# A 2 KB output by two DMAs of neighbouring partitions instead of one DMA of four strided partitions

## The chip, the cores and the metric

The kernel runs on one core of one Trainium2 chip. The time is device time in microseconds (us) of that core; medians of several executions are given. "Span" is the time from the first to the last instruction in the profiled execution; it is some 1.8 us shorter than the device time. Times inside a span count from its start. A run is called fast when it is not over 1.5% above the fastest of its kernel; all the runs below are, but where a kernel ran only once its state is unknown.

Engines: TensorE (PE), VectorE (DVE), ScalarE (ACT), GpSimd (POOL) and SyncE (SP). DMAs are issued here by SyncE (queue q1 in the trace) and by ScalarE (queue q10).

## The reference, cut to what matters

One token goes through attention over a long cache and through a gated MLP, and a gate mixes the two:

```python
x = A_x                                              # (1, 1, 1024)
g = sigmoid((x * gate_w).sum(-1, keepdims=True))
a = A_ref(x, A_k_cache, A_v_cache, A_wq, A_wo)       # 32 heads, 4 kv heads, 65536 keys
b = B_ref(x, B_w_in, B_w_sp, B_b_sp, B_w_out)
return g * a + (1 - g) * b                           # (1, 1, 1024), bfloat16: 2 KB
```

All the inputs that are read come to 162 MB. The output is 2 KB.

## The kernel before

The last product, with `A_wo`, is accumulated in one tile `out_ps` of PSUM (the memory that TensorE writes its products to), of 128 partitions by 256 columns. The 1024 outputs are cut into four blocks of 256; block t fills partitions 32t to 32t+31, and all 32 partitions of a block hold the same values, because the vector is broadcast to 32 columns of weights.

```python
P, B, NB = 128, 32, 4
WO_SPLIT = ((16,), (8, 4, 2, 1, 1))     # columns of A_wo per load
...
NO = D // NB                            # 256
out_ps = psl.tile([P, NO], FP32, name="out_ps")

def project(w, n, vec, c0, first=False, last=False):
    for c in range(n):
        for t in range(NB):
            nc.tensor.matmul(
                out_ps[t * B:(t + 1) * B, :],
                lhsT=vec[:, c0 + c:c0 + c + 1].to_broadcast([P, B]),
                rhs=w[:, c, t * NO:(t + 1) * NO], ...)
...
for split in WO_SPLIT:
    ...
    for n in split:
        nc.sync.dma_start(out=t[:, c0 - b:c0 - b + n, :], in_=wo_view[:, c0:c0 + n, :])
        project(t[:, c0 - b:c0 - b + n, :], n, oa, c0, last=(c0 + n == OC))
        c0 += n
out_sb = const.tile([P, NO], BF16, name="out_sb")
nc.scalar.copy(out=out_sb[:], in_=out_ps[:])
nc.scalar.dma_start(out=out.rearrange("o t (q n) -> (o t q) n", n=NO), in_=out_sb[::B, :])
```

`out_sb[::B, :]` takes partitions 0, 32, 64 and 96: one row of each block, 512 B each. After that nothing is left but the program's closing waits, drains and barriers.

Of the kernel before, what the change touches and what calls it, by code (L numbers as in the profile page):

```python
# [17 lines left out]
B = 32  # L18
# [9 lines left out]
def kernel(  # L28
# [15 lines left out]
    nc = tc.nc  # L44
# [127 lines left out]
    for t in range(2):  # L172
        nc.vector.tensor_tensor(
            out=xm[:, t], in0=xb_ps[:, t * P:(t + 1) * P].rearrange("p (i c) -> p c i", c=KC),
# [51 lines left out]
    for hf in range(2):  # L226
        nc.vector.tensor_tensor(  # L227
            out=zm[:, hf], in0=z_ps[:, hf * HN:hf * HN + ZN].rearrange("p (j c) -> p j c", c=FC),
# [3 lines left out]
                            in_=zm.rearrange("p h j c -> p h c j"), axis=AX.X, op=ALU.add)  # L232
# [44 lines left out]
    for k in range(NHB):  # L277
        xs = slice(k * NX // NHB, (k + 1) * NX // NHB)
        nc.vector.tensor_tensor(  # L279
            out=qm[:, xs], in0=q_ps[:, k * HN:(k + 1) * HN].rearrange("p (x j e) -> p x j e",  # L280
                                                                   j=B, e=2),
# [6 lines left out]
        out=q4[:], in0=q1[:].rearrange("p x e -> p (x e)").unsqueeze(1).to_broadcast(  # L288
            [P, NB, NX * 2]),
# [7 lines left out]
    for g in range(G):  # L297
        k, t0 = g * T2 // NB, g * T2 % NB
        nc.vector.tensor_copy(out=qs[:, g].rearrange("p b (t h) -> p b t h", t=T2),
                              in_=qv[:, k, t0:t0 + T2].rearrange("p t h b -> p b t h"))  # L300
# [107 lines left out]
    NO = D // NB  # L408
# [35 lines left out]
    for split in WO_SPLIT:  # L444
        t = kv.tile([P, CT * P], BF16, name="wo_t", tag="kv")
        t = t[:].rearrange("p (c n) -> p c n", n=D)
        b = c0
        for n in split:
            nc.sync.dma_start(out=t[:, c0 - b:c0 - b + n, :], in_=wo_view[:, c0:c0 + n, :])  # L449
            project(t[:, c0 - b:c0 - b + n, :], n, oa, c0, last=(c0 + n == OC))  # L450
            c0 += n
    out_sb = const.tile([P, NO], BF16, name="out_sb")
    nc.scalar.copy(out=out_sb[:], in_=out_ps[:])  # L453
    nc.scalar.dma_start(out=out.rearrange("o t (q n) -> (o t q) n", n=NO), in_=out_sb[::B, :])

    last = {}
    for ins in list(nc.cur_bb.bb.instructions):
# [36 lines left out]
```

## Time and profile before

| | before |
|---|---|
| device time, median | 385.78 us (385.75 to 385.80) |
| span of the profiled run | 383.92 us |
| load queue q1, share of 16 engines | 98.5% |
| from the start of the last cast to the end of the span | 2.90 us, 0.75% of the time |

From the page of the kernel before: the row of DMA busy tenths over 40 slices of the span, the load queue, and the chain that ended last by engine.

```profile
DMA  8999999999999999999999999999999999999995
q1 hardware_dynamic: 6192, 162.01, 98.5%
DMA 60%; DVE 20%; PE 11%; issue 5%; ACT 2%; SPq 1%; DVEq 0%; ACTq 0%
```

The kernel is bound by its loads until its last slice. Only there does anything else count. The end of the timeline of the kernel before (start us, duration us, engine, line, operation, what ended the idle time before it; ACTq is ScalarE's sequencer, issuing a DMA):

```profile
380.69 0.29 PE L414 MATMUL out_ps<-wo_t,oa 128*32 128x256 bf16 x4 [0.36 <-DMA wo_t<-in_A_wo_dram]
381.02 0.37 ACT L453 CAST out_sb<-out_ps 128x256 bf16<-128x256 f32 x1 [47.61 <-PE out_ps L414]
381.43 0.61 ACTq L454 DMA_DIRECT2D out_dram<-out_sb  x1
```

The last load's matmuls are followed by the cast, and that by one issue of 0.61 us. From the waits of SyncE's queue, before (what was waited for, total us, times, longest us):

```profile
SPq L489 <- DMA out_dram<-out_sb: 2.4, 1, 2.4
```

SyncE holds the program open until the output has landed. The packet and landing records of the trace split this end.

These are ScalarE's first four DMAs, of 8, 8, 1 and 1 rows:

```profile
0.74 0.61 ACTq L117 DMA_DIRECT2D xg<-in_A_x_dram  x1
1.39 0.29 ACTq L118 DMA_DIRECT2D xg<-in_gate_w_dram  x1
1.71 0.27 ACTq L120 DMA_DIRECT2D wb<-in_B_w_sp_dram  x1
2.00 0.27 ACTq L121 DMA_DIRECT2D wb<-in_B_b_sp_dram  x1
```

### The profile page before, as it was taken

The numbers are of one execution on the slowest core, as the hardware profiler recorded it, in microseconds if no ns is written. First come the engines' busy times: TensorE is split into PE (matmuls) and PEld (weight loads), VectorE is DVE, ScalarE is ACT, GpSimd is POOL, SyncE is SP. The second block draws the span as 40 slices with busy tenths as digits, with TensorE's granted clock in tenths as the row PEclk, the third lists the DMA queues.
The fourth block names the chain that finished last, engine by engine and source line by source line (L and its number), as shares of the span: only waits on it lengthen the run. The fifth ranks groups of instructions, "written<-read, shape, count | busy, mean of one in ns | idle before, by whom it ended". The sixth has DMA issues, their size and how long they took to land.

```text
span 383.9 us, 2650 instructions
## 1 busy us (share of the span) xinstructions
PE 242.3 (63%) x1372; PEld 59.3 (15%) x796; DVE 218.5 (57%) x211; ACT 39.6 (10%) x55; POOL 4.4 (1%) x10
## 2 busy tenths in 40 slices
PE   0433447976449948466699393774993937685553
PEld 0110001111202201011121020121220201121122
DVE  5141478988497563658975545679754546730040
ACT  1010001100511101014011010140110101400000
POOL 4000000000000000000000000000000000000000
PEclk9996559889659989686599797865997869888868
DMA  8999999999999999999999999999999999999995
GB/s 335 430 437 437 435 434 430 423 431 426 428 427 437 435 430 437 427 434 430 423 432 427 437 437 422 430 434 437 427 425 427 437 438 427 425 430 431 434 411 203
DMA packets 6248, 162.18 MB, mean 422 GB/s; under 512 B 728, under 2 KB 732, under 8 KB 1116
## 3 DMA queue, kind: packets, MB, share of 16 engines
q1 hardware_dynamic: 6192, 162.01, 98.5%
q8 instruction: 8, 0.13, 0.1%
q14 instruction: 4, 0.03, 0.0%
q10 hardware_dynamic: 44, 0.01, 0.0%
HBM read 162.01 MB, written 0.00 MB: 422 GB/s over the span
## 4 chain that ended last, share of the span: by engine, by line
DMA 60%; DVE 20%; PE 11%; issue 5%; ACT 2%; SPq 1%; DVEq 0%; ACTq 0%
DMA kn<-in_A_k_cache_dram 47%; DVE kt L320 16%; DMA wo_t<-in_A_wo_dram 8%; PE s_ps L326 8%; DMA win_t<-in_B_w_in_dram 5%; DVE pt L362 2%; PE o_ps L372 2%; ACT sc L337 1%; PE z_ps L213 1%; ACT sc L359 1%; DVE mx L341 1%; DVE o_sb L387 0%; SPq L449 0%; ACT L359 0%; PE nb_ps L352 0%
## 5 line engine op out<-in xcount | busy, mean ns | idle before, releaser
L326 PE MATMUL s_ps<-kt,wt 128*128 128x512 bf16 x512 | 142.3, 437 | 67.9 <-DVE kt L320 67.3
L320 DVE STREAM_TRANSPOSE kt<-kn 128x2048 int32<-128x2048 int32 x64 | 143.3, 2284 | 63.5 <-DMA kn<-in_A_k_cache_dram 63.4
L372 PE MATMUL o_ps<-vt,pt 128*64 128x512 bf16 x512 | 69.2, 432 | 8.8 <-DMA vt<-in_A_v_cache_dram 8.8
L326 PEld LDWEIGHTS <-wt 128*128 128x128 bf16 x256 | 27.6, 108 | 184.0 <-issue 122.9
L337 ACT CAST sc<-s_ps 128x1024 bf16<-128x1024 f32 x16 | 16.2, 1013 | 253.8 <-PE s_ps L326 253.8
L372 PEld LDWEIGHTS <-pt 128*64 128x64 bf16 x256 | 17.2, 124 | 57.9 <-issue 56.4
L362 DVE STREAM_TRANSPOSE pt<-sc 128x1024 bf16<-128x1024 bf16 x16 | 18.6, 1218 | 6.8 <-ACT sc L359 6.8
L383 DVE TENSOR_TENSOR om<-o_ps,own 128x1024 f32<-128x1024 f32 x4 | 4.8, 1205 | 26.8 <-PE o_ps L372 26.8
L359 ACT ACTIVATE sc<-sc,nb 128x1024 bf16<-128x1024 bf16 x16 | 18.2, 1139 | 10.2 <-DVE nb L355 10.2
L322 DVE TENSOR_REDUCE mx<-sc 128x1 f32<-128x1024 bf16 x12 | 14.3, 1192 | 4.4 <-ACT sc L337 4.4
L341 DVE TENSOR_REDUCE mx<-sc 128x1 f32<-128x1024 bf16 x4 | 4.9, 1220 | 12.3 <-ACT sc L337 12.3
L213 PE MATMUL q_ps<-wq_t,xT 128*32 128x512 bf16 x64 | 7.2, 630 | 7.3 <-DMA wq_t<-in_A_wq_dram 7.3
L393 PE MATMUL om_ps<-o_sb,hsel 128*32 128x128 f32 x8 | 2.4, 398 | 13.6 <-DVE o_sb L387 13.6
L213 PE MATMUL z_ps<-win_t,xT 128*32 128x448 bf16 x64 | 6.4, 577 | 4.9 <-DMA win_t<-in_B_w_in_dram 4.9
L414 PE MATMUL out_ps<-wo_t,oa 128*32 128x256 bf16 x128 | 6.3, 346 | 4.6 <-DMA wo_t<-in_A_wo_dram 3.2
L279 DVE TENSOR_TENSOR rowt<-q_ps,own_b 128x512 f32<-128x512 f32 x2 | 1.3, 686 | 12.4 <-PE q_ps L213 12.4
L345 PE MATMUL mt_ps<-ident_f,m 128*1 128x128 f32 x4 | 1.4, 346 | 10.2 <-DVE m L343 10.2
L387 DVE TENSOR_REDUCE o_sb<-om 128x128 f32<-128x1024 f32 x4 | 7.5, 1871 | 0.1
L227 DVE TENSOR_TENSOR rowt<-z_ps,own_b 128x448 f32<-128x448 f32 x2 | 1.2, 620 | 9.6 <-PE z_ps L213 9.6
L213 PEld LDWEIGHTS <-xT 128*32 128x32 bf16 x64 | 3.0, 140 | 20.3 <-issue 20.3
L453 ACT CAST out_sb<-out_ps 128x256 bf16<-128x256 f32 x1 | 0.4, 372 | 47.6 <-PE out_ps L414 47.6
L414 PEld LDWEIGHTS <-oa 128*32 128x32 bf16 x128 | 4.2, 119 | 6.9 <-issue 4.2
(88 smaller groups left out, 57.9 us busy)
## 6 DMA issues: line engine op xcount, KB each, us to landing
kn<-in_A_k_cache_dram SPq DMA_DIRECT2D x16, 4096.0 KB, 26.5
vt<-in_A_v_cache_dram SPq DMA_DIRECT2D x16, 4096.0 KB, 32.9
wq_t<-in_A_wq_dram SPq DMA_DIRECT2D x2, 4096.0 KB, 28.4
win_t<-in_B_w_in_dram SPq DMA_DIRECT2D x2, 3584.0 KB, 15.1
wo_t<-in_A_wo_dram SPq DMA_DIRECT2D x1, 4096.0 KB, 27.2
wout_t<-in_B_w_out_dram SPq DMA_DIRECT2D x1, 3584.0 KB
wo_t<-in_A_wo_dram SPq DMA_DIRECT2D x1, 2048.0 KB
wo_t<-in_A_wo_dram SPq DMA_DIRECT2D x1, 1024.0 KB
```

Of the source, the lines that this page charges most:

```text
L213: ins = nc.tensor.matmul(ps[t * B:(t + 1) * B, k * HN:k * HN + n], lhsT=xT[:, i * KH + c:i * KH + c + 1].to_broadcast([P, B]), rhs=w[:, c, ...
L320: nc.vector.transpose(out=kt[:].bitcast(I32), in_=kb[:, v * n:(v + 1) * n])
L322: nc.vector.reduce_max(**late.pop())
L326: ins = nc.tensor.matmul(s_ps[:, k * HN:(k + 1) * HN], lhsT=wt[g % 2][:, v, b].rearrange("p a v h -> p (a v h)"), rhs=kx[:, b // 2, b % 2, ...
L337: nc.scalar.copy(out=sct[g, j][:], in_=s_ps[:])
L341: nc.vector.reduce_max(**late.pop())
L359: nc.scalar.activation(out=sct[g, j][:], in_=sct[g, j][:], func=ACT.Exp, scale=SCALE, bias=nb[:, 0:1], accum_out=lss[g][:, j:j + 1])
L362: nc.vector.transpose(out=ptt[g, j][:].rearrange("p c x -> p (c x)"), in_=sct[g, j][:])
L372: ins = nc.tensor.matmul(o_ps[g][hs, e, :], lhsT=ptt[g, j][:, 2 * u:2 * u + 2, :].rearrange("p c x -> p (c x)"), rhs=vx[:, 2 * u + e], sta ...
L383: nc.vector.tensor_tensor(out=om8[:], in0=o_ps[g][:].rearrange("p e (v d) -> p (e v) d", d=DH), in1=own_8[:].unsqueeze(2).to_broadcast([P, ...
L387: nc.vector.tensor_reduce(out=o_sb[:], in_=om8[:].rearrange("p x d -> p d x"), axis=AX.X, op=ALU.add)
L414: nc.tensor.matmul(out_ps[t * B:(t + 1) * B, :], lhsT=vec[:, c0 + c:c0 + c + 1].to_broadcast([P, B]), rhs=w[:, c, t * NO:(t + 1) * NO], st ...
```

## The change

The intent is a shorter way out for the output: partitions 31 and 32 are neighbours and belong to blocks 0 and 1, partitions 95 and 96 to blocks 2 and 3. So two DMAs of two neighbouring partitions each replace one of four strided partitions, and two engines issue them at the same time.

```diff
     out_sb = const.tile([P, NO], BF16, name="out_sb")
+    out_rows = out.rearrange("o t (q n) -> (o t q) n", n=NO)
     nc.scalar.copy(out=out_sb[:], in_=out_ps[:])
-    nc.scalar.dma_start(out=out.rearrange("o t (q n) -> (o t q) n", n=NO), in_=out_sb[::B, :])
+    for i, queue in enumerate((nc.scalar, nc.sync)):
+        p0 = (2 * i + 1) * B - 1
+        queue.dma_start(out=out_rows[2 * i:2 * i + 2, :], in_=out_sb[p0:p0 + 2, :])
```

It mixes three things: neighbours instead of strided partitions, two rows per DMA instead of four, and a second queue.

## The prediction

> **What bounds the kernel.** The stream of loads. By the page's DMA part, queue q1 is busy 98.5% of 16 engines' span and moves 162 MB at a mean of 422 GB/s; the slices stay at 9 tenths until the last. The chain of waits gives DMA 60%, DVE 20%, PE 11%. The change leaves that alone: only the output DMA differs in any engine's order of instructions.
>
> **The only part the change can reach is the end of the program**, read from the timeline, the groups of the output line and the packet records (us from the span's start):
>
> - 380.69: last four matmuls of out_ps; 381.02 to 381.39: ScalarE casts 128x256 into out_sb.
> - 381.43 to 382.04: ScalarE issues the output DMA, 0.61 us.
> - 382.67 to 382.76: its packets run on q10: four of 512 B and four of 4 B.
> - about 383.05 to 383.09: its landings; 383.11: SyncE, which waited for it, goes on (the waits of the DMA queue: 2.4 us on the output).
> - 383.11 to 383.92: closing drains and barriers, 0.8 us.
>
> So the output costs 1.7 us from issue to landing, of which moving the data is under 0.1 us. All of it is 0.4% of 385.78 us.
>
> **What the change does to it.** ScalarE's issue now names two rows instead of four. The start of the trace says that rows hardly count: ScalarE's first issue (8 rows) took 0.61 us, the next (8 rows) 0.29, the two of one row 0.27 each. The 0.61 of the output looks like a first issue after a long pause (381 us), not four rows; I estimate 0.59 to 0.61 afterwards. SyncE adds an issue of 0.33 to 0.44 us (its loads of wo_t and the cache), which starts after the same cast, in parallel, and ends about 0.2 us earlier than ScalarE's.
>
> The Trainium skill, "DMA: Bandwidth & Descriptors", section "Issuing engines are not separate DMA queues", says that issuing from several engines only saves sequencer time and that the copies run on the same 16 engines. Here there is no sequencer time to save: one issue still follows the cast on ScalarE. Its section "Why a DMA increments its semaphore by 16 and not by 1" says that a copy uses as many engines as divide its slowest dimension; this trace agrees (four data packets and four 4 B packets for four rows; eight and eight for eight). So I expect two and two in each of q10 and q1, on the same two engines, which costs perhaps 0.03 to 0.07 us more (a 512 B packet took 0.031 to 0.036 us).
>
> **Sum.** ScalarE's issue 0 to -0.02 us; packets sharing two engines 0 to +0.07; a second landing for SyncE to wait for 0 to +0.05. All on the critical path: about +0.02 us, nothing. Predicted 385.8 us, 8 times in 10 within 385.4 to 386.2; faster by over 2%: 0.005, within 2%: 0.99, slower by over 2%: 0.005.
>
> **What would show it.** Right: ScalarE's output issue near 0.6 us, SyncE's near 0.35 to 0.45, starting within 0.1 us of each other; last packet 0.6 to 0.8 us after ScalarE's issue ends; SyncE goes on 1.6 to 1.8 us after the cast; everything before the cast as before.
>
> **What would make it wrong.** An issue whose time goes with rows or partition stride (then up to 0.3 us faster); two sequencers that issue at once delaying each other (slower by 0.1 to 0.4 us); or a load stream that differs between builds by some tenths of a us.

## The result

The changed kernel ran at 385.53 us (median of 4 runs, 385.39 to 385.56), the kernel before in the same rounds at 385.79 us (4 runs, 385.75 to 385.88). Ratios are the mean time of one kernel's fast runs over the mean of the other's fast runs in the same rounds, so not quite the ratio of the medians; here it is 0.9992, with a 95% interval of 0.9978 to 1.0006. By the 2% measure the kernels are the same. The interval includes 1, yet the two sets of runs do not overlap, and the repeat in experiment e5 shows the same (in a second repeat, e12, the sets overlap a little), so I treat the 0.26 us as real and look for it in the trace.

The load-bound part did not change. The same lines of the page after:

```profile
DMA  8999999999999999999999999999999999999995
q1 hardware_dynamic: 6196, 162.01, 98.5%
DMA 64%; DVE 20%; PE 8%; issue 6%; ACT 1%; SPq 0%; ACTq 0%; DVEq 0%
```

q1 has four packets more, the output's two of 512 B and two of 4 B. The end of the timeline after:

```profile
380.71 0.41 PE L414 MATMUL out_ps<-wo_t,oa 128*32 128x256 bf16 x4 [0.25 <-DMA wo_t<-in_A_wo_dram]
381.16 0.37 ACT L454 CAST out_sb<-out_ps 128x256 bf16<-128x256 f32 x1 [47.93 <-PE out_ps L414]
381.56 0.33 SPq L457 DMA_DIRECT2D out_dram<-out_sb  x1
381.56 0.26 ACTq L457 DMA_DIRECT2D out_dram<-out_sb  x1
```

ScalarE's issue fell from 0.61 to 0.26 us: that is the surprise. From the waits of SyncE's queue, after:

```profile
SPq L457 <- ACT out_sb L454: 20.6, 1, 20.6
SPq L492 <- DMA out_dram<-out_sb: 0.8, 1, 0.8
```

SyncE now waits for the cast before it can issue, and its wait for the landing is short only because it begins later.

The last matmuls begin within 0.02 us of each other in the two profiles but took 0.41 us instead of 0.29. Both durations also occur in later profiles of kernels whose matmuls are the same, so this is not the change's doing. I therefore measure from the start of the cast. A landing is the update of a semaphore by which a DMA tells that its data has arrived. The landings are from the semaphore records, the packets from the DMA records of each trace:

| from the start of the cast, us | before | after | difference |
|---|---|---|---|
| cast, until the first output issue starts | 0.403 | 0.399 | -0.004 |
| first issue starts, until the first packet | 1.244 | 0.748 | -0.496 |
| first packet starts, until the last has ended | 0.098 | 0.071 | -0.027 |
| last packet, until the last landing | 0.320 | 0.476 | +0.156 |
| last landing, until the end of the span | 0.830 | 0.928 | +0.098 |
| sum | 2.895 | 2.622 | -0.273 |

The sum agrees with the 0.26 us of the timed runs. (The spans of the two profiled runs, 383.92 and 383.78 us, differ by 0.14 only, because the last matmuls took 0.12 longer in the second.) Half a microsecond is saved at the start of the transfer, and half of that is given back at its end. The experiments ask what each half is due to.

### The profile page after: what moved, and what is told of

It reads as the page before. It is cut to its first block, busy times and chain, and to the rows that moved or that the text cites. A ratio compares the mean times of both kernels' runs of the same rounds, so it can differ in the third digit from the quotient of the medians.

```text
span 383.8 us, 2652 instructions
## 1 busy us (share of the span) xinstructions
PE 234.1 (61%) x1372; PEld 57.7 (15%) x796; DVE 218.3 (57%) x211; ACT 39.6 (10%) x55; POOL 4.4 (1%) x10
## 4 chain that ended last, share of the span: by engine, by line
DMA 64%; DVE 20%; PE 8%; issue 6%; ACT 1%; SPq 0%; ACTq 0%; DVEq 0%
DMA kn<-in_A_k_cache_dram 53%; DVE kt L320 17%; DMA wo_t<-in_A_wo_dram 8%; PE s_ps L326 4%; PE o_ps L372 2%; DMA wb<-in_B_b_sp_dram 2%; DVE pt L362 1%; PE z_ps L213 1%; ACT sc L337 1%; DVE o_sb L387 0%; SPq L449 0%; ACT sc L359 0%; DVE mx L341 0%; DVE om L383 0%; DVE mx L322 0%
## 5 line engine op out<-in xcount | busy, mean ns | idle before, releaser
L326 PE MATMUL s_ps<-kt,wt 128*128 128x512 bf16 x512 | 136.5, 420 | 74.9 <-DVE kt L320 74.7
L372 PE MATMUL o_ps<-vt,pt 128*64 128x512 bf16 x512 | 68.2, 427 | 6.8 <-DMA vt<-in_A_v_cache_dram 6.8
L326 PEld LDWEIGHTS <-wt 128*128 128x128 bf16 x256 | 26.6, 104 | 186.0 <-issue 121.6
```

What stands on the lines that cost most here:

```text
L326: ins = nc.tensor.matmul(s_ps[:, k * HN:(k + 1) * HN], lhsT=wt[g % 2][:, v, b].rearrange("p a v h -> p (a v h)"), rhs=kx[:, b // 2, b % 2, ...
L372: ins = nc.tensor.matmul(o_ps[g][hs, e, :], lhsT=ptt[g, j][:, 2 * u:2 * u + 2, :].rearrange("p c x -> p (c x)"), rhs=vx[:, 2 * u + e], sta ...
```

## The experiments

Theory "stride": the step between the source's partitions makes the issue long; neighbours are cheap, whatever the number of rows or queues. Rival "rows": two rows are cheaper than four. Rival "pause": a lone issue after a long pause is slow, and SyncE's company ends that. A further rival is that the second engine makes the gain. The edits are against the kernel before; `out_rows` is as in the change.

### e1 to e4: strided or not, how many rows, after what pause

e1, split alone, still strided:

```diff
-    nc.scalar.dma_start(out=out.rearrange(...), in_=out_sb[::B, :])
+    for i, queue in enumerate((nc.scalar, nc.sync)):
+        queue.dma_start(out=out_rows[2 * i:2 * i + 2, :],
+                        in_=out_sb[2 * i * B:(2 * i + 1) * B + 1:B, :])
```

> Two DMAs as in the change, from ScalarE and SyncE, but of two strided partitions each (0, 32 and 64, 96); the result stays correct. Theory stride (a step of 32 partitions in the source makes the issue long): ScalarE's issue 0.55 to 0.61 us, SyncE's above 0.5, time 385.8. Rival rows (the issue goes with the number of rows, 4 rows 0.61, 2 rows 0.26): 0.26 and 0.33, time 385.5. Rival pause (a lone first issue after a long pause is long, SyncE's company ends that): 0.26 and 0.33, time 385.5.

Measured: 386.05 us (385.93 to 386.20; before on this chip: 385.83, 385.73 to 386.04, 7 runs). The timeline of e1:

```profile
381.72 0.63 SPq L456 DMA_DIRECT2D out_dram<-out_sb  x1
381.73 0.60 ACTq L456 DMA_DIRECT2D out_dram<-out_sb  x1
```

Two rows, two engines, and both issues take 0.6 us. Rows and pause fall, and so does the second engine. The split alone is even a loss of 0.2 us by the medians, though the sets of runs overlap, and of 0.19 us in the trace. No theory had put that down: SyncE's first packet came 0.59 us after its issue ended, ScalarE's 0.89 us after its own, and the two sets of packets ran 0.27 us apart. Two strided DMAs issued at once seem to be worked off one after the other; only this one trace shows it.

e2, neighbours alone:

```diff
-    nc.scalar.dma_start(out=out.rearrange(...), in_=out_sb[::B, :])
+    nc.scalar.dma_start(out=out_rows[:, :], in_=out_sb[B - 2:B + 2, :])
```

> One DMA from ScalarE of four neighbouring partitions (30 to 33): wrong output on purpose, rows 0,0,1,1. Theory stride: issue 0.26 to 0.30 us, time 385.3 to 385.5. Rival rows: issue 0.61, time 385.8. Rival pause: issue 0.61, time 385.8.

Measured: 385.39 us (385.22 to 385.49), output wrong. The timeline of e2:

```profile
381.64 0.27 ACTq L455 DMA_DIRECT2D out_dram<-out_sb  x1
```

Four rows cost 0.27 us to issue when they are neighbours. Only the stride theory allows it. The last packet landed after 0.326 us and the end came 0.830 us later, as before: with one DMA nothing is given back, and from cast to end it is 2.404 us.

e3, the kernel before with another small load shortly ahead of the output:

```diff
     out_sb = const.tile([P, NO], BF16, name="out_sb")
+    again = big.tile([P, 2 * VC, DH], FP32, name="om8")
+    nc.scalar.dma_start(out=again[0:KC, 0, 0:P // 2].bitcast(BF16),
+                        in_=gate_w.rearrange("(k i) -> k i", i=P))
     nc.scalar.copy(out=out_sb[:], in_=out_ps[:])
```

> The kernel before with one more small load (8 rows of 256 B) issued by ScalarE about 12 us before the output. Theory stride: the output issue stays 0.61 us, time 385.8; the small load itself, rows neighbouring, 0.26 to 0.30 even after a pause of about 367 us. Rival rows: output 0.61, 385.8. Rival pause: the small load is the long one (0.6), the output issue falls to 0.27 to 0.29, time 385.4 to 385.5.

Measured: 385.94 us. ScalarE's timeline in e3:

```profile
370.64 0.28 ACTq L454 DMA_DIRECT2D om<-in_gate_w_dram  x1
381.04 0.37 ACT L456 CAST out_sb<-out_ps 128x256 bf16<-128x256 f32 x1 [47.84 <-PE out_ps L414]
381.44 0.61 ACTq L458 DMA_DIRECT2D out_dram<-out_sb  x1
```

The load is eight neighbouring rows after a pause of 368 us, and takes 0.28 us. The output, 11 us later, still takes 0.61. A pause costs nothing. The 0.6 us of the very first issue in every run must have another cause, at the program's start; no experiment asked which. e3 also lost 0.1 us by the medians, which the expectation did not have. Its runs (385.87 to 386.07) overlap those of the kernel before, but in its trace the end came 0.934 us after the last landing instead of 0.830.

e4, the strided DMA from SyncE:

```diff
-    nc.scalar.dma_start(out=out.rearrange(...), in_=out_sb[::B, :])
+    nc.sync.dma_start(out=out_rows[:, :], in_=out_sb[::B, :])
```

> The one DMA of four strided partitions, issued by SyncE, which has issued loads up to some 30 us before. Theory stride: SyncE's issue 0.6 to 0.7 us, time 385.8 to 385.9. Rival rows: the same, 0.6 to 0.7. Rival pause: 0.33 to 0.44, time 385.5 to 385.6.

Measured: 385.80 us. The timeline of e4:

```profile
381.48 0.64 SPq L455 DMA_DIRECT2D out_dram<-out_sb  x1
```

The strided issue takes 0.64 us on SyncE, 0.61 on ScalarE: it is long on either engine.

### e5 and e12: the changed kernel again

> The changed kernel once more, with five rounds: is its gain of 0.26 us real? If the stride theory holds, 385.4 to 385.6 us against 385.75 to 385.95 of the kernel before on this chip; ScalarE's issue again 0.26, SyncE's 0.33; SyncE goes on 1.7 to 1.8 us after the cast begins. If the gain was luck, the medians come within 0.1 us.

> The changed kernel beside e11 on the same chip: 385.45 to 385.6 us.

Measured: e5 385.55 us (385.51 to 385.61, 5 runs) against 385.89 (385.78 to 385.97, 9 runs); e12 385.60 us (385.53 to 385.81) against 385.83 (385.73 to 386.38). The ratios are 0.9992 and 0.9994. From cast to end it was 2.624 and 2.619 us, after 2.622 in the first profile. The gain is small but it repeats: 0.26, 0.34 and 0.23 us by the medians. The 95% interval of the ratio includes 1 each time, and in e12 the two sets of runs overlap, so its size is best read from the trace.

### e6 and e7: neighbours without the second queue

e6, both pairs from ScalarE:

```diff
-    nc.scalar.dma_start(out=out.rearrange(...), in_=out_sb[::B, :])
+    for i in range(2):
+        p0 = (2 * i + 1) * B - 1
+        nc.scalar.dma_start(out=out_rows[2 * i:2 * i + 2, :], in_=out_sb[p0:p0 + 2, :])
```

> The two pairs of neighbours both from ScalarE, one after the other: it takes SyncE's part away. Theory stride (the gain is the neighbours, not the second engine): issues 0.26 to 0.28 each, the second ends 0.26 later than in the changed kernel, SyncE goes on 1.75 to 2.0 us after the cast begins, time 385.5 to 385.75. Rival (the second engine makes the gain): no gain, 385.8 or more.

Measured: 385.63 us (385.49 to 385.67), before 385.89. From the lines of e6 by source line (durations min/median/max ns, then first and last start):

```profile
L457 ACTq DMA_DIRECT2D out_dram<-out_sb x2: 253/260/267, 381.5 to 381.8; - x2
```

So half of the gain in the trace stays without SyncE: 2.752 us from cast to end, 0.14 less than before and 0.13 more than with two queues. By the medians it is more, 0.26 of the 0.34 us. In this kernel the second pair's packets ran 0.31 us after the first pair's, and the last landing came 0.327 us after the last packet, with no extra delay.

e7, a correct output by one DMA of neighbours. Two casts lay blocks 2 and 3 beside blocks 0 and 1 in the same partitions:

```diff
-    out_sb = const.tile([P, NO], BF16, name="out_sb")
-    nc.scalar.copy(out=out_sb[:], in_=out_ps[:])
-    nc.scalar.dma_start(out=out.rearrange(...), in_=out_sb[::B, :])
+    half = P // 2
+    out_sb = const.tile([half, 2, NO], BF16, name="out_sb")
+    nc.scalar.copy(out=out_sb[:, 0, :], in_=out_ps[0:half, :])
+    nc.scalar.copy(out=out_sb[:, 1, :], in_=out_ps[half:P, :])
+    nc.scalar.dma_start(out=out.rearrange("o t (b q n) -> (o t q) b n", b=2, n=NO),
+                        in_=out_sb[B - 1:B + 1, :, :])
```

> Correct output by ONE DMA of two neighbouring partitions: two casts of 64x256 on ScalarE put blocks 2 and 3 beside blocks 0 and 1 in the same partitions, then one DMA of 2x2 rows from ScalarE. Theory stride: issue 0.26 to 0.35; the second cast costs 0.2 to 0.35 more; only one landing, so the wait from last packet to SyncE is 0.34 to 0.36 us instead of 0.54; time 385.5 to 385.75, between the two kernels. Rival rows: issue 0.6, time 386.0 to 386.2.

Measured: 385.62 us (385.58 to 385.70). The timeline of e7:

```profile
381.17 0.37 ACT L454 CAST out_sb<-out_ps 64x256 bf16<-64x256 f32 x1 [47.38 <-PE out_ps L414]
381.54 0.37 ACT L455 CAST out_sb<-out_ps 64x256 bf16<-64x256 f32 x1
381.94 0.27 ACTq L456 DMA_DIRECT2D out_dram<-out_sb  x1
```

The rows on the DRAM side are strided here, and the issue still takes 0.27 us: strided rows there cost nothing in this case. The second cast costs 0.37 us, which more than eats what the single landing saves. From the last cast's start to the end it was 2.378 us, from the first cast's start 2.755.

### e8 and e9: how far, and on which side

e8 takes partitions 0, 2, 4 and 6 (`in_=out_sb[0:8:2, :]`, wrong output). e9 is e3 with the small load going into eight partitions with a step of 8 (`out=again[0:8 * KC:8, ...]`).

> One DMA from ScalarE of four partitions with a step of 2 (0, 2, 4, 6): wrong output on purpose. If any step other than 1 makes the issue long: 0.6 us, 385.8. If only steps across blocks of 32 do: 0.27 us, 385.4.

> The extra small load of e3 again, but into eight partitions with a step of 8 instead of eight neighbours. If the step counts on either side of a DMA, its issue takes 0.6 to 0.7 us instead of 0.28; if only in the source, 0.28. The output's issue stays 0.61 in either case.

Measured: e8 385.92 us (before 385.89), e9 one run (385.88, before 385.84; states unknown). The issue lines of the timelines, e8 first, then e9's load:

```profile
381.40 0.70 ACTq L455 DMA_DIRECT2D out_dram<-out_sb  x1
```

```profile
370.43 0.69 ACTq L454 DMA_DIRECT2D om<-in_gate_w_dram  x1
```

A step of 2 is no cheaper than one of 32 (0.70 us against 0.61), and a load into strided partitions takes 0.69 us where the same load into neighbours took 0.28 (e3). So the cost goes with a partition step other than 1 in on-chip memory, in either direction. With steps of 2, 8 and 32, the seven strided issues (leaving out the kernel before) lie between 0.58 and 0.71 us.

### e10: one half of the changed output alone

```diff
-    nc.scalar.dma_start(out=out.rearrange(...), in_=out_sb[::B, :])
+    nc.sync.dma_start(out=out_rows[2:4, :], in_=out_sb[3 * B - 1:3 * B + 1, :])
```

> Only SyncE's half of the changed output (rows 2 and 3; rows 0 and 1 are not written, wrong on purpose), without ScalarE's. In the changed kernel SyncE's queue took 0.48 us from its last packet to its last landing, ScalarE's 0.34. Theory company (two DMAs that arrive together on the same two engines): 0.33 to 0.35 here, SyncE goes on 1.55 to 1.6 us after the cast begins. Rival (SyncE's queue lands later by itself): 0.48.

Measured (one run of each, states unknown, half of the output not written): 385.25 us, before 385.84. SyncE's issue again took 0.33 us, but the last landing came 0.327 us after the last packet, not 0.476, and the end 0.824 us after that. SyncE's queue is not slow by itself. In the three profiles of the changed kernel the delay is 0.468 to 0.476 us; in e1 and e6, where the two sets of packets run 0.27 and 0.31 us apart, it is 0.317 and 0.327. So the extra 0.15 us comes with two DMAs that arrive together. What in the chip makes the second wait is not shown.

### e11: a version meant to beat both

The last two columns of `A_wo` are loaded by half of the output instead of by column, so that the folded cast of e7 can run while the last load is still under way:

```diff
-WO_SPLIT = ((16,), (8, 4, 2, 1, 1))
+WO_SPLIT = ((16,), (8, 4, 2))
+TAIL = 2
...
+    for h in (1, 0):
+        cols = slice(h * D // 2, (h + 1) * D // 2)
+        nc.sync.dma_start(out=t[:, c0 - b:c0 - b + TAIL, cols], in_=wo_view[:, c0:c0 + TAIL, cols])
+        project(..., blocks=(2 * h, 2 * h + 1))
+        nc.scalar.copy(out=out_sb[:, h, :], in_=out_ps[h * P // 2:(h + 1) * P // 2, :])
```

with the DMA of e7 after it.

> A version meant to beat both, correct output: the last two columns of A_wo come in two loads by half of the output instead of by column, the half of blocks 2 and 3 first, so that its cast (folded into the partitions of blocks 0 and 1, 0.37 us in e7) is done while the last load lands; then the last matmuls, the other cast, and one DMA of two neighbouring partitions from ScalarE. If the theory holds (neighbours 0.27 us to issue, one landing and not two in company): SyncE goes on 1.54 to 1.60 us after the last cast begins, against 1.75 in the changed kernel; time 385.3 to 385.45 us, 0.1 to 0.25 below the changed kernel. If the first cast holds up the last matmuls (they share the bank and wait for it) or the half loads land later, it is spent again: 385.5 or more.

Measured: 385.99 us (385.56 to 389.27, 6 runs); ratio 1.0014, interval 0.9989 to 1.0039. It does not beat either kernel. The run of 389.27 us had a granted clock of 0.63 against 0.79 to 0.85 in all other runs beside it; the ratio includes it, but I leave it out of any comparison of sizes. Without it the mean of e11 is 385.89 us, the same as that of the kernel before beside it. The other five, 385.56 to 386.27, scatter more widely than the changed kernel's (385.53 to 385.81). The profile fell on the slow-clock run, so only its local order can be read. The timeline of e11:

```profile
384.27 0.37 ACT L459 CAST out_sb<-out_ps 64x256 bf16<-64x256 f32 x1 [45.71 <-PE out_ps L415]
384.69 0.39 PE L415 MATMUL out_ps<-wo_t,oa 128*32 128x256 bf16 x4 [0.46 <-ACT out_sb L459]
385.12 0.36 ACT L459 CAST out_sb<-out_ps 64x256 bf16<-64x256 f32 x1 [0.48 <-PE out_ps L415]
385.51 0.27 ACTq L460 DMA_DIRECT2D out_dram<-out_sb  x1
```

The tail is as expected: 2.374 us from the last cast's start to the end. But the last matmuls waited for the first cast, as the expectation feared. The last load had landed at 384.50, and they began at 384.69, where the kernel before began its own 0.04 us after the landing. That gives back about 0.15 us. The rest of the loss, and the scatter, stay open: no undisturbed profile of e11 exists.

### All runs side by side

"Cast to end" is from the start of the (first output) cast to the end of the span, in the one execution that was profiled; the difference is to the kernel before (2.895). e5 and e12 are the changed kernel again (2.624 and 2.619), and e11 has no undisturbed profile.

| kernel | longest output issue, us | cast to end, us | difference | time minus before, medians |
|---|---|---|---|---|
| after | 0.33 | 2.622 | -0.27 | -0.26 |
| e1, two DMAs, strided | 0.63 | 3.084 | +0.19 | +0.22 |
| e2, one DMA, neighbours (wrong) | 0.27 | 2.404 | -0.49 | -0.44 |
| e3, before with another load | 0.61 | 3.010 | +0.12 | +0.11 |
| e4, strided, SyncE | 0.64 | 2.870 | -0.03 | -0.03 |
| e6, two pairs, ScalarE | 0.27 | 2.752 | -0.14 | -0.26 |
| e7, folded, one DMA | 0.27 | 2.755 | -0.14 | -0.27 |
| e8, step of 2 (wrong) | 0.71 | 2.999 | +0.10 | +0.03 |
| e9, e3 with a strided load | 0.58 | 2.980 | +0.09 | +0.04 |
| e10, half of the output | 0.33 | 2.352 | -0.54 | -0.59 |

The last two columns agree within 0.13 us, so the end of the program accounts for the differences to that measure.

### What is given back at the end

The last row of the result's table, +0.098 us, is told apart by the closing waits. The time from the last landing to the end is either 0.82 to 0.83 us (before, e1, e2, e4, e7, e8, e10, e11) or 0.93 us (after, e3, e5, e6, e9, e12). The two differ in SyncE's instruction records: in the second group one more semaphore wait of SyncE stands after the last landing (two instead of one). e3 and e9 have only one output DMA and pay it too, so it goes with the place of the awaited semaphore in the closing list, not with the second DMA as such. SyncE's records list that order: semaphore 100 is awaited two instructions before 110, which is in the last wait of the list. In all profiles of the first group the last landing is on 110, in all of the second on 100. e1 comes nearest to a test: it has two DMAs on the engines and semaphores of the change, but there ScalarE's DMA, on 110, landed last, and the end took 0.825 us. No experiment moved that place alone, and whether the other order would win the 0.1 us back was not tried.

## Why the prediction was right or wrong

- **The bound: right.** The loads set all but the last 3 us. The prediction's upper limit, that the whole output is worth 0.4%, held, and 385.53 us lies within 385.4 to 386.2.
- **"I estimate 0.59 to 0.61 afterwards" for ScalarE's issue: wrong.** It took 0.26 us. This is the step that failed. The prediction took 0.61 us for "a first issue after a long pause", because the program's very first issue takes 0.61 as well. e3 shows 0.28 after a pause of 368 us. The cause is the partition step (e1, e2, e8). The prediction compared rows but not the partition step of ScalarE's first four DMAs: their on-chip side is in neighbouring partitions, and the output's is not.
- **"Here there is no sequencer time to save": wrong for the same reason.** From the issue's start to the first packet, 0.50 us went away, 0.35 of it within ScalarE's issue. The Trainium skill, "DMA: Bandwidth & Descriptors", section "Issuing engines are not separate DMA queues", says that several issuing engines only save issue time. That agrees: with two queues instead of one (after against e6) the packets end 0.27 us sooner after the cast, about one issue of ScalarE; 0.15 of it is lost again at the landing, so 0.13 us is left.
- **SyncE's issue, 0.33 to 0.44 us, starting within 0.1 us: right.** 0.33 us, 0.004 us earlier than ScalarE's.
- **Two and two packets on each queue: right**, as the skill's section "Why a DMA increments its semaphore by 16 and not by 1" (same page) leads one to expect: two of 512 B and two of 4 B on q10 and on q1. **"Packets sharing two engines 0 to +0.07" was mis-sized**: the packets themselves were 0.03 us shorter in total. Which DMA engines carried them the trace does not show.
- **"A second landing for SyncE to wait for 0 to +0.05": mis-sized.** The two DMAs that arrive together cost 0.156 us at the landing. The closing waits took 0.098 us more, which goes with the awaited semaphore's place and not with the second DMA as such; that is 0.25 us together.
- **The signs it named.** "Last packet 0.6 to 0.8 us after ScalarE's issue ends" measured 0.56 (the skill, same page, section "Latency and other measured facts", gives some 600 ns to the first byte, without saying from which point; here the first packet started 0.49 us after ScalarE's issue ended for neighbours and 0.63 for strided partitions). "SyncE goes on 1.6 to 1.8 us after the cast" measured 1.38 from the end of the cast. Both misses go with the neighbours, which shortened the issue and also the stretch from its end to the first packet.
- **What would make it wrong: named.** "An issue whose time goes with rows or partition stride (then up to 0.3 us faster)" is what happened, with stride and not rows.

The sum was +0.02 us and measured -0.27 us. That the measured time lies in the predicted range is luck and not a sign that the mechanism was right: the range, 0.4 us to either side, was wider than the whole effect that the prediction had missed.

## What to carry to other kernels

When a small DMA ends a program, look at its issue in the timeline and at the partition step of its on-chip side: 0.6 us against 0.27 was the sign of a step other than 1 (only ScalarE's very first issue took 0.6 us without one), and a duplicate row in a neighbouring partition may be there to take instead. Prefer one such DMA to two that arrive together, where the one costs no further work; splitting without making the rows neighbours loses. Account for an ending by its pieces (issue, packets, landing, closing waits), as a saving in one may be half given back in the next.

## What the Trainium skill lacked or had wrong

- "DMA: Bandwidth & Descriptors" has nothing on what an on-chip partition step other than 1 costs at issue: 0.58 to 0.71 us against 0.25 to 0.33 us for the output's neighbours on either issuing engine, for steps of 2, 8 and 32, at 2, 4 and 8 rows; and for the output 0.14 us more from ScalarE's issue end to its first packet (0.63 against 0.49).
- The same page, "Latency and other measured facts", gives one figure of some 600 ns for the first byte, for any source and without the point that it counts from; the runs show 0.43 (SyncE, e10) to 0.49 us (ScalarE) from the end of an issue to its first packet for neighbours, and 0.59 to 0.64 for strided partitions when one DMA ran alone.
- The same page, in its rules for kernel authors, says that spreading DMAs over several issuing engines does not help bandwidth; it does not say that two small stores that arrive together land later: 0.47 us from last packet to last landing against 0.32 to 0.33 for one alone.
- No page that was looked up has what one more closing wait after the last landing costs: 0.93 us to the end instead of 0.82 to 0.83.
